# Attention and two expert layers on one core: elementwise work of the weight conversions moved from GpSimd to VectorE and ScalarE

## The chip, the cores and the metric

The kernel runs on one core of a Trainium2 chip. Its time is the device time of one execution in microseconds (us). The engines are TensorE (PE in the profile, PEld for its weight loads), VectorE (DVE), ScalarE (ACT), GpSimd (POOL) and SyncE (SP); each takes its own instructions in order, and they wait for each other by semaphores. All inputs and outputs lie in HBM, working data in SBUF, products of TensorE in PSUM.

## The reference

Three layers follow each other; nothing but their shapes and formulas matters here.

```python
# 1: attention, batch 4, 8 heads, 512 local + 32 global positions, head size 64
s_l = concat(q_l @ k_g.T, where(|i-j| <= 32, q_l @ k_l.T, -1e9)) / 8 ; out_l = softmax(s_l) @ [v_g; v_l]
s_g = q_g @ [k_g; k_l].T / 8                                         ; out_g = softmax(s_g) @ [v_g; v_l]
# 2: 2304 tokens x 512 -> 2048 -> 512;  w_in, w_out arrive as 64-bit floats
h = x @ w_in ; g = h if h >= 1, 0 if h <= -1, else (h+1)**2 / 4 ; x = g @ w_out
# 3: 8 experts, one per token (argmax), only tokens with x @ w_skip > 0
out = x + gate * (relu(x @ w1[e]) @ w2[e])
```

The matrices of layers 2 and 3 are multiplied in three products, high x high, high x low and low x high, where high is a value rounded to TensorE's fast float format (fp32r) and low is what is left.

## The kernel before

**Attention (lines 189 to 441).** 64 steps `s`, eight for each of the 8 pairs of heads. In a step TensorE makes scores ahead (L252), transposes probabilities (L290) and multiplies with the values (L305). VectorE masks and reduces (`reduce_max`, L261), adds, inverts and scales (L275, L279, L284), and copies the output out of PSUM (L308). ScalarE takes exponentials (L268) and copies the transposes (L291). GpSimd copies the columns of the global queries into the transposed tile (`global_columns`, L296). Scores are up to five steps ahead of values. An explicit table, `calls`, says at which step a generator takes its next piece: `globals_` for the global queries of the next pair, and `convert` for a slice of weights.

**Conversion of weights (`convert`, L88 to L106).** `w_in` and `w_out` are 64-bit floats, of which a slice of 128x512 is loaded as pairs of 32-bit words. Each of the 32 conversions (16 slices of either) is a generator with six pieces:

1. SP loads the raw words (L91).
2. ScalarE scales the upper words (L94); VectorE scales and rounds the lower words (L95).
3. VectorE masks the sign (L97), shifts and joins (L98).
4. GpSimd adds the rounded lower words (L101), as integers.
5. ScalarE rounds to the high part (L104).
6. GpSimd subtracts it, which gives the low part (L106).

Eight slices of `w_in` and two of `w_out` are converted in attention, the others in the first unit of layer 2.

**Layer 2 (`stage1`, `middle`, `stage2`, L151, L509, L527; main loop L712).** The tokens are cut into five units of 512, 512, 512, 384 and 256; a unit has 16 steps, one for each slice of 128 of the inner size. Iteration `m` issues `stage1(m)` (12 products, L158), `stage2(m-1)` (12 products in the first three units, L533) and `middle(m)`: ScalarE's relu and square (L513, L514), VectorE's clamp (L517, which reads PSUM), ScalarE's rounding to `gh` (L518) and VectorE's subtraction for `gl` (L522). In unit 0 `middle` also drives the conversions by `advance(age)`, which takes the next piece of every conversion of that age. `conversions(m)` ages all of them by one and starts those of `STARTS`; a conversion does pieces 2 to 4 in the middle of the third iteration after its start, and pieces 5 and 6 one iteration later. Six iterations have two conversions at either age. In each step `stage2` goes over the token tiles `q` and does, for each, two products with `gh` and one with `gl`.

`split_x` (L127) makes the high and low parts of the next unit's tokens: ScalarE rounds (L138), an engine given as an argument subtracts (L139). That is VectorE for units 1 to 4 and GpSimd for unit 0, whose four parts are made in steps 20, 28, 36 and 44 of attention.

**Layer 3 (L734 to the end).** Tokens are routed while layer 2 runs. The rows of an expert's tokens are gathered and scattered by GpSimd's indirect DMAs (L641, L707), in blocks of 256 rows; branches (`tc.If`) leave out blocks and experts without tokens. While an expert's products run, `products` (L823) splits the 16 slices of the next expert's weights with `split` (L630): ScalarE rounds, VectorE subtracts, and for slices 5, 8, 11 and 14 GpSimd does.

Of the kernel before, what the change touches and what calls it, by code (L numbers as in the profile page):

```python
# [7 lines left out]
F32 = mybir.dt.float32  # L8
# [39 lines left out]
def tile_kernel(ctx, tc, q, k, v, w_in, w_out, wsg, w1, w2,  # L48
# [39 lines left out]
    def convert(raw, cvt, src, parts):  # L88
        flat = raw.rearrange("p a b -> p (a b)")
        low, high = raw[:, :, 0], raw[:, :, 1]  # L90
        nc.sync.dma_start(out=flat, in_=src.bitcast(I32))  # L91
        yield
        t = cvt() if callable(cvt) else cvt
        nc.scalar.activation(out=t.bitcast(F32), in_=high.bitcast(F32), func=AF.Copy, scale=2.0 ** -112)  # L94
        nc.vector.tensor_scalar(out=low, in0=low.bitcast(U32), scalar1=2.0 ** -29, scalar2=None, op0=ALU.mult)  # L95
        yield
        nc.vector.tensor_scalar(out=high, in0=high, scalar1=-(1 << 31), scalar2=None, op0=ALU.bitwise_and)  # L97
        nc.vector.scalar_tensor_tensor(out=t, in0=t, scalar=3, in1=high, op0=ALU.logical_shift_left,  # L98
                                       op1=ALU.bitwise_or)
        yield  # L100
        nc.gpsimd.tensor_tensor(out=t, in0=t, in1=low, op=ALU.add)  # L101
        yield
        hi, lo = parts()
        nc.scalar.activation(out=hi, in_=t.bitcast(F32), func=AF.Copy)  # L104
        yield
        nc.gpsimd.tensor_tensor(out=lo, in0=t.bitcast(F32), in1=hi.bitcast(F32), op=ALU.subtract)  # L106

    def convert_in(raw, t, f):
        return convert(raw, t, w_in[:, f, :], lambda: (winH[f], winL[f]))
# [14 lines left out]
    tiles = [(b, j) for b in range(B) for j in range(NJ)] + [None]  # L124
    units = [[0, 1, 2, 3], [4, 5, 6, 7], [8, 9, 10, 11], [12, 13, 14], [15, 16]]

    def split_x(u, part=range(4), low=nc.vector):  # L127
        tl = [tiles[i] for i in units[u]]
        loc = [x for x in tl if x]
        for c in part:  # L130
            o = 0
            pieces = [(xT[loc[0][0]][:, c, loc[0][1]:loc[0][1] + len(loc), 0:128], 128 * len(loc), 128)]
            if len(loc) < len(tl):
                pieces.append((xg[:, c], 128, SG))
            for src, m, w in pieces:
                hv = xh[c][:, o:o + m].rearrange("p (j c) -> p j c", c=w)
                lv = xl[c][:, o:o + m].rearrange("p (j c) -> p j c", c=w)
                nc.scalar.activation(out=hv, in_=src, func=AF.Copy)  # L138
                low.tensor_tensor(out=lv, in0=src, in1=hv.bitcast(F32), op=ALU.subtract)  # L139
                o += m  # L140


# [3 lines left out]
    def wo(hl, f):  # L146
        return (woutH, woutL)[hl][f // 4][:, f % 4, :]
# [24 lines left out]
    def advance(age, n=1):  # L172
        for c in pipe:
            if c[0] == age:
                for _ in range(n):
                    next(c[1], None)
# [12 lines left out]
    with tc.tile_pool(name="att", bufs=1) as a1:  # L189
# [206 lines left out]
        for s in range(NS + 1):  # L396
            n, i8 = divmod(s, 8)
            if s < NS:
                if i8 == 1 and 1 <= n and n + 1 < NG:
                    load(V_b, v, n + 1)  # L400
                if i8 == 3 and n + 2 < NG:
                    load(K_b, k, n + 2)
                    load_q(n + 2)
                transposes(s)
            for r in range(ahead, min(s + AHEAD + 1, ahead + 2, NS + 1)):
                if r < NS:
                    scores(r)
                softmax(r, r - 1)
                if r < NS:
                    exps(r)  # L410
                ahead = r + 1
            if s >= 1:
                values(s - 1)
            for g in calls[s]:
                next(g, None)
            if s % 8 == 4 and 2 <= n < 6:
                split_x(0, [n - 2], nc.gpsimd)
            if s + 2 < NS:
                global_columns(s + 2)

            if s == NS - 13:

                sp2 = wp.tile([128, 2, 512, 2], I32, tag="B2", name="sp2")
                sp2t = sp2[:, 1].rearrange("p a b -> p (a b)")[:, 0:512]
                sp0 = wp.tile([128, 2, 512, 2], I32, tag="B0", name="sp0")
                plan(convert_out(sp0[:, 0], cvts[0], 0), *(NS - x for x in (11, 7, 6, 5, 4, 3)))
                plan(convert_out(sp2[:, 0], sp2t, 1), *(NS - x for x in (12, 5, 4, 3, 2, 1)))
            if s == NS - AHEAD:
                sp3 = wp.tile([128, 2, 512, 2], I32, tag="B3", name="sp3")
                raws += [sp3[:, 0], sp3[:, 1]]  # L430
                h_ps += [bank(i, f"h{i}") for i in range(2)]
                conversions(-2)
            if s == NS - 1:
                sp7 = wp.tile([128, 2, 512, 2], I32, tag="B7", name="sp7")
                raws += [sp7[:, 0], sp7[:, 1]]
                conversions(-1)
            if NS - 4 <= s < NS:
                stage1(0, [s - NS + 4])
# [70 lines left out]
    def middle(m):  # L509
        u, f = divmod(m, NF)  # L510
        n = 128 * len(units[u])
        hp, t, (a, b_) = h_ps[m % 2][:, 0:n], tb[m % 2][:, 0:n], gs(m)
        nc.scalar.activation(out=t, in_=hp, func=AF.Relu, bias=half, scale=0.5)  # L513
        nc.scalar.activation(out=t, in_=t, func=AF.Square)  # L514
        if u == 0:
            advance(4)
        nc.vector.scalar_tensor_tensor(out=t, in0=t, scalar=1.0, in1=hp, op0=ALU.min, op1=ALU.max)  # L517
        nc.scalar.activation(out=a, in_=t, func=AF.Copy)  # L518
        if u == 0:
            advance(4)  # L520
            advance(3)
        nc.vector.tensor_tensor(out=b_, in0=t, in1=a.bitcast(F32), op=ALU.subtract)  # L522
        if u == 0:
            advance(3)
            advance(3)

    def stage2(m):  # L527
        u, f = divmod(m, NF)
        gH, gL = gs(m)
        for q in range(len(units[u])):  # L530
            s = slice(128 * q, 128 * q + 128)
            for k, (lg_, rw) in enumerate(((gH, wo(0, f)), (gH, wo(1, f)), (gL, wo(0, f)))):
                nc.tensor.matmul(y_ps[q], lhsT=lg_[:, s], rhs=rw, start=(f == 0 and k == 0),  # L533
                                 stop=(f == NF - 1 and k == 2))

    def store(u):
        for q, i in enumerate(units[u]):
# [89 lines left out]
        src = (w1, w2)[i // 4][bass.ds(e, 1), :, (i % 4) * 1024:(i % 4) * 1024 + 1024]  # L627
        nc.sync.dma_start(out=raws[i], in_=src.rearrange("a p c -> (a p) c"), cond=cond)

    def split(q, f, raw, low=nc.vector):  # L630
        r = raw[:, 512 * (f % 2):512 * (f % 2) + 512]
        hi, lo = Wt[q][0][f], Wt[q][1][f]
        nc.scalar.activation(out=hi, in_=r, func=AF.Copy)
        low.tensor_tensor(out=lo, in0=r, in1=hi.bitcast(F32), op=ALU.subtract)

    def load_ids(addr):
        nc.gpsimd.dma_start(out=nid, in_=table[bass.ds(addr, BLK), :].rearrange("(s p) c -> p s c", s=2))
# [184 lines left out]

    def products(k, many, pre):  # L823
        q = k % 2
        todo = [(1 - q, f, raws[f // 2], nc.gpsimd if f > 4 and f % 3 == 2 else nc.vector)
                for f in range(NF)] if pre else []

        def splits(n=1):
            for _ in range(n):
                if todo:  # L830
                    split(*todo.pop(0))

        if many:
            nc.vector.tensor_copy(out=cyg_, in_=nyg_)
            for f in range(NEF):
                mm1(q, f)
                if f == 1:
                    load_rows()
                    if pre:
                        prefetch(k + 1, range(4 if k == 0 else 2, 8))  # L840
                if f >= (0 if k == 0 else 5):
                    splits()
            nc.vector.tensor_copy(out=pid, in_=cid[:, :, 0:2])
            for s_ in range(2):
                transpose_rows(s_)
            for s_ in range(2):
                for f in range(NEF):
                    mm2(q, s_, s_, f)
                    if f % 2 == 1:
                        splits()  # L850
                if s_ == 0:
                    finish_rows(0)
                    send_rows(0)
        else:
            nc.vector.tensor_copy(out=cyg_[:, 1], in_=nyg_[:, 0])
            load_rows()
            if pre:
                prefetch(k + 1, range(4 if k == 0 else 2, 8))
            mm1_few(q, 0)
            splits(1 if k == 0 else 0)  # L860
            mm1_few(q, 1, range(2))
            transpose_few(0)
            mm1_few(q, 1, range(2, 4))
            nc.vector.tensor_copy(out=pid[:, 1], in_=cid[:, 0, 0:2])
            splits()
            for f in range(NEF):
                mm2(q, 0, 1, f)
                if f == 1:
                    transpose_few(1)
                if f in (2, 3):  # L870
                    transpose_rows(f - 2)
                splits(2 if f % 2 == 0 else 1)
        splits(NF)
# [147 lines left out]
```

## Time and profile before

The median of three timed executions is 743.02 us (742.79 to 744.99). The execution that was profiled took 745.22 us, of which the profile spans 743.5.

| engine | busy us | share of the span |
|---|---|---|
| TensorE, products | 690.8 | 93% |
| TensorE, weight loads | 565.2 | 76% |
| VectorE | 438.5 | 59% |
| ScalarE | 366.4 | 49% |
| GpSimd | 183.5 | 25% |

Matmuls are pipelined and their ends are modelled, so a busy TensorE is not one at its peak. The busy time of an instruction runs from its start to its end as recorded, and holds what it spent standing in between. The share of an engine over the whole span hides that the stages differ; attention lasts until about 155 us, the first unit of layer 2 until about 256, and the experts begin at about 564. The chain of waits that ends last has 55% of its time on TensorE, 16% on VectorE, 9% on DMAs and 8% in "issue", which is time in which an engine waited for nothing that the profile shows.

### The profile page before, as it was taken

How to read it: one execution, taken by the hardware profiler on the slowest of the kernel's cores; microseconds unless marked ns; L12 is line 12 of the kernel's file. 1: busy time of each engine (PE TensorE's matmuls, PEld its weight loads, DVE VectorE, ACT ScalarE, POOL GpSimd, SP SyncE). 2: the span in 40 equal slices, each digit the busy share in tenths (PEclk: the TensorE clock that was granted, in tenths of full speed). 3: DMA queues.
4: the chain of work that ended last, by engine and by line, in shares of the span. 5: the costliest groups of instructions: out<-in, count | busy, mean ns of one | idle time of the engine just before them, and what ended most of it. 6: DMA issues, size and time to landing. Idle time of an engine off the chain costs nothing.

```text
span 743.5 us, 11769 instructions
## 1 busy us (share of the span) xinstructions
PE 690.8 (93%) x4081; PEld 565.2 (76%) x4081; DVE 438.5 (59%) x1375; ACT 366.4 (49%) x872; POOL 183.5 (25%) x210
## 2 busy tenths in 40 slices
PE   6999999899788999999999999999999999999743
PEld 4777777678565777788777888889888799988632
DVE  6899999978999643333434344434666574223801
ACT  4878888855545543335433354445664162112501
POOL 2143333446677300000000000110001343222320
PEclk9999999999999999999999999999999999999957
DMA  9756566323441030000300006021301361114510
GB/s 249 238 170 165 180 178 197 114 86 115 140 118 52 0 114 1 0 1 1 113 1 1 1 0 227 1 58 56 115 1 57 96 218 60 58 37 119 195 47 15
DMA packets 28244, 66.85 MB, mean 90 GB/s; under 512 B 3755, under 2 KB 12589, under 8 KB 27108
## 3 DMA queue, kind: packets, MB, share of 16 engines
q1 hardware_dynamic: 25092, 58.41, 25.2%
q0 software_dynamic: 3040, 7.10, 3.2%
q8 instruction: 51, 0.84, 0.5%
q14 instruction: 61, 0.50, 0.2%
HBM read 53.38 MB, written 12.43 MB: 89 GB/s over the span
## 4 chain that ended last, share of the span: by engine, by line
PE 55%; DVE 16%; DMA 9%; issue 8%; ACT 3%; POOL 2%; POOLq 0%; DVEq 0%; ACTq 0%
PE h L158 21%; PE y L533 21%; DMA nyg<-ys,nid 6%; PE e L663 4%; PE z L698 3%; DVE P_a L284 3%; DVE gl L522 2%; DMA out_dram<-ob,pid 2%; PE o L305 1%; DVE P_a L261 1%; DVE sp L95 1%; ACT P_a L268 1%; PE t L290 1%; DVE cvt L98 1%; DVE cvtm L98 1%
## 5 line engine op out<-in xcount | busy, mean ns | idle before, releaser
L533 PE MATMUL y<-wout,gh 128*128 128x512 f32 x544 | 173.9, 401 | 2.6 <-ACT gh L518 2.5
L533 PEld LDWEIGHTS y<-wout,gh 128*128 128x128 f32 x544 | 100.3, 191 | 25.1 <-ACT gh L518 5.3
L158 PE MATMUL h<-xh,winH 128*128 128x512 f32 (+2 forms) x320 | 118.6, 370 | 0.0
L533 PE MATMUL y<-wout,gl 128*128 128x512 f32 x272 | 109.0, 401 | 7.9 <-DVE gl L522 7.8
L158 PE MATMUL h<-xh,winL 128*128 128x512 f32 (+2 forms) x320 | 114.8, 359 | 0.0
L158 PE MATMUL h<-xl,winH 128*128 128x512 f32 (+2 forms) x320 | 114.5, 358 | 0.0
L517 DVE SCALAR_TENSOR_TENSOR tb<-tb,h 128x512 f32<-128x512 f32 (+2 forms) x80 | 48.5, 606 | 102.9 <-ACT tb L514 102.2
L500 POOL DMA_INDIRECT table<-ids,slot x17 | 17.4, 1024 | 301.7 <-DVE slot L498 298.8
L513 ACT ACTIVATE tb<-h,misc 128x512 f32<-128x512 f32 (+2 forms) x80 | 49.6, 620 | 78.4 <-PE h L158 66.1
L522 DVE TENSOR_TENSOR gl<-tb,gh 128x512 fp32r<-128x512 f32 (+2 forms) x80 | 59.5, 743 | 47.5 <-ACT gh L518 47.4
L533 PEld LDWEIGHTS y<-wout,gl 128*128 128x128 f32 x272 | 51.8, 190 | 23.6 <-DVE gl L522 12.5
L158 PEld LDWEIGHTS h<-xh,winH 128*128 128x128 f32 x320 | 60.3, 188 | 11.0 <-issue 2.7
L518 ACT ACTIVATE gh<-tb 128x512 fp32r<-128x512 f32 (+2 forms) x80 | 45.2, 565 | 44.6 <-DVE tb L517 44.6
L158 PEld LDWEIGHTS h<-xh,winL 128*128 128x128 f32 x320 | 60.3, 189 | 7.9
L158 PEld LDWEIGHTS h<-xl,winH 128*128 128x128 f32 x320 | 60.5, 189 | 7.4
L268 ACT ACTIVATE P_a<-P_a,st 128x160 f32<-128x160 f32 x128 | 53.7, 421 | 22.1 <-DVE st L261 20.9
L698 PE MATMUL z<-WA,h 128*128 128x512 f32 x240 | 57.9, 394 | 0.0
L305 PE MATMUL o<-PT,V 128*64 128x160 f32 x512 | 49.5, 314 | 4.1 <-ACT PT L291 1.9
L698 PEld LDWEIGHTS z<-WA,h 128*128 128x128 f32 x240 | 44.2, 188 | 8.7
L663 PE MATMUL e<-yTH,WA 128*128 128x256 f32 x256 | 48.7, 286 | 0.2
L252 PE MATMUL s<-K,Q 128*128 128x160 f32 x256 | 46.5, 305 | 1.2 <-DVE st L261 0.7
L514 ACT ACTIVATE tb<-tb 128x512 f32<-128x512 f32 (+2 forms) x80 | 45.5, 568 | 2.5
(203 smaller groups left out, 1204.2 us busy)
## 6 DMA issues: line engine op xcount, KB each, us to landing
xr<-in_w_dram SPq DMA_DIRECT2D x24, 512.0 KB, 6.6
V<-in_v_dram SPq DMA_DIRECT2D x8, 1024.0 KB, 4.9
K<-in_k_dram SPq DMA_DIRECT2D x7, 800.0 KB, 5.7
raw<-in_w_in_dram SPq DMA_DIRECT2D x10, 512.0 KB, 6.5
sp<-in_w_out_dram SPq DMA_DIRECT2D x10, 512.0 KB, 3.9
ys<-xT SPq DMA_DIRECT2D x15, 256.0 KB, 2.9
out_dram<-xT SPq DMA_DIRECT2D x15, 256.0 KB, 3.9
Q<-in_q_dram SPq DMA_DIRECT2D x14, 256.0 KB, 7.0
```

Of the source, the lines that this page charges most:

```text
L158: nc.tensor.matmul(hp, lhsT=lw, rhs=rx[:, 0:n], start=(c == 0 and k == 0), stop=(c == 3 and k == 2))
L252: nc.tensor.matmul(s_ps[s % 2][:, a, 0:W], lhsT=Q_b[n % 2][:, i, j, :, :, a].rearrange("p h c -> p (h c)"), rhs=K_b[n % 2][:, i, W * j + 9 ...
L268: nc.scalar.activation(out=px(s, a), in_=px(s, a), func=AF.Exp, bias=st[:, a:a + 1], scale=-1.0, accum_out=st[:, 2 + a:3 + a])
L305: nc.tensor.matmul(o[64 * h:64 * h + 64, 0:W], lhsT=V[:, j, t, i * 128 + h * 64:i * 128 + h * 64 + 64], rhs=PT[:, t, h, :], start=(t == 0) ...
L513: nc.scalar.activation(out=t, in_=hp, func=AF.Relu, bias=half, scale=0.5)
L514: nc.scalar.activation(out=t, in_=t, func=AF.Square)
L517: nc.vector.scalar_tensor_tensor(out=t, in0=t, scalar=1.0, in1=hp, op0=ALU.min, op1=ALU.max)
L518: nc.scalar.activation(out=a, in_=t, func=AF.Copy)
L522: nc.vector.tensor_tensor(out=b_, in0=t, in1=a.bitcast(F32), op=ALU.subtract)
L533: nc.tensor.matmul(y_ps[q], lhsT=lg_[:, s], rhs=rw, start=(f == 0 and k == 0), stop=(f == NF - 1 and k == 2))
L663: nc.tensor.matmul(hp, lhsT=lw, rhs=ry[:, c], start=(n == 0), stop=(n == 11))
L698: nc.tensor.matmul(z_ps[z], lhsT=lh[:, d], rhs=rw, start=(f == 0 and k == 0), stop=(f == NEF - 1 and k == 2))
```

## The change

In `convert`, the rounding of the lower words goes from VectorE to ScalarE, the addition and the subtraction from GpSimd to VectorE. The subtractions of `split_x` and `split` that were GpSimd's go to VectorE. In `middle` the pieces of the conversions are put in another order: pieces 5 and 6 of the older ones stay ahead of the subtraction for `gl`, pieces 2 to 4 of the younger ones all come behind it. `stage2` does all products with `gh` of a step first, and those with `gl` after them.

```diff
@@ convert
-        nc.vector.tensor_scalar(out=low, in0=low.bitcast(U32), scalar1=2.0 ** -29, scalar2=None, op0=ALU.mult)
+        nc.scalar.activation(out=low, in_=low.bitcast(U32), func=AF.Copy, scale=2.0 ** -29)
...
-        nc.gpsimd.tensor_tensor(out=t, in0=t, in1=low, op=ALU.add)
+        nc.vector.tensor_tensor(out=t, in0=t, in1=low, op=ALU.add)
...
-        nc.gpsimd.tensor_tensor(out=lo, in0=t.bitcast(F32), in1=hi.bitcast(F32), op=ALU.subtract)
+        nc.vector.tensor_tensor(out=lo, in0=t.bitcast(F32), in1=hi.bitcast(F32), op=ALU.subtract)
@@ split_x
-    def split_x(u, part=range(4), low=nc.vector):
+    def split_x(u, part=range(4)):
...
-                low.tensor_tensor(out=lv, in0=src, in1=hv.bitcast(F32), op=ALU.subtract)
+                nc.vector.tensor_tensor(out=lv, in0=src, in1=hv.bitcast(F32), op=ALU.subtract)
@@ attention
-                split_x(0, [n - 2], nc.gpsimd)
+                split_x(0, [n - 2])
@@ middle
         nc.scalar.activation(out=a, in_=t, func=AF.Copy)
         if u == 0:
             advance(4)
-            advance(3)
         nc.vector.tensor_tensor(out=b_, in0=t, in1=a.bitcast(F32), op=ALU.subtract)
         if u == 0:
             advance(3)
             advance(3)
+            advance(3)
@@ stage2
-        for q in range(len(units[u])):
-            s = slice(128 * q, 128 * q + 128)
-            for k, (lg_, rw) in enumerate(((gH, wo(0, f)), (gH, wo(1, f)), (gL, wo(0, f)))):
-                nc.tensor.matmul(y_ps[q], lhsT=lg_[:, s], rhs=rw, start=(f == 0 and k == 0),
-                                 stop=(f == NF - 1 and k == 2))
+        for lows in (False, True):
+            for q in range(len(units[u])):
+                s = slice(128 * q, 128 * q + 128)
+                for hl in range(1 if lows else 2):
+                    nc.tensor.matmul(y_ps[q], lhsT=(gL if lows else gH)[:, s], rhs=wo(hl, f),
+                                     start=(f == 0 and hl == 0 and not lows), stop=(f == NF - 1 and lows))
@@ split
-    def split(q, f, raw, low=nc.vector):
+    def split(q, f, raw):
...
-        low.tensor_tensor(out=lo, in0=r, in1=hi.bitcast(F32), op=ALU.subtract)
+        nc.vector.tensor_tensor(out=lo, in0=r, in1=hi.bitcast(F32), op=ALU.subtract)
@@ products
-        todo = [(1 - q, f, raws[f // 2], nc.gpsimd if f > 4 and f % 3 == 2 else nc.vector)
-                for f in range(NF)] if pre else []
+        todo = [(1 - q, f, raws[f // 2]) for f in range(NF)] if pre else []
```

## Rows read from the trace of the kernel before

**Rows 1.** Windows: length, each engine's busy time (instructions), granted clock, DMA share, GB/s.

```profile
34.70:122.20 87.50, 83.08 (x726) 65.06 (x724) 85.12 (x417) 73.26 (x245) 31.48 (x54) 1.00 0.60 170
122.20:155.30 33.10, 30.36 (x245) 22.51 (x239) 29.75 (x120) 23.47 (x70) 15.50 (x22) 0.95 0.41 148
161.50:247.90 86.40, 76.10 (x303) 57.75 (x301) 79.78 (x87) 46.90 (x80) 58.26 (x42) 0.96 0.32 98
247.90:577.00 329.10, 328.83 (x1776) 273.68 (x1777) 144.05 (x462) 152.13 (x302) 24.15 (x23) 1.00 0.13 42
577.00:743.50 166.50, 138.14 (x817) 120.71 (x815) 68.82 (x141) 43.27 (x92) 46.23 (x47) 0.93 0.30 94
```

**Rows 2.** Order of time, VectorE, one iteration: start, duration, line, operands, preceding idle.

```profile
222.02 0.67 DVE L517 SCALAR_TENSOR_TENSOR tb<-tb,h 128x512 f32<-128x512 f32 x1
222.62 2.58 DVE L95 TENSOR_SCALAR sp<-sp 128x512 int32<-128x512 uint32 x2
225.12 1.76 DVE L522 TENSOR_TENSOR gl<-tb,gh 128x512 fp32r<-128x512 f32 x1
...
227.26 0.69 DVE L98 SCALAR_TENSOR_TENSOR cvtm<-cvtm,sp 128x512 int32<-128x512 int32 x1
...
228.33 1.66 DVE L98 SCALAR_TENSOR_TENSOR cvtm<-cvtm,sp 128x512 int32<-128x512 int32 x1
229.91 0.68 DVE L517 SCALAR_TENSOR_TENSOR tb<-tb,h 128x512 f32<-128x512 f32 x1
```

**Rows 3.** Order of time, GpSimd, the same stretch.

```profile
222.18 1.31 POOL L101 TENSOR_TENSOR cvt<-cvt,raw 128x512 int32<-128x512 int32 x1 [0.63 <-DVE cvt L98]
223.45 1.47 POOL L106 TENSOR_TENSOR wout<-cvt,wout 128x512 fp32r<-128x512 f32 x1
224.87 1.46 POOL L106 TENSOR_TENSOR winL<-cvt,winH 128x512 fp32r<-128x512 f32 x1
228.03 1.41 POOL L101 TENSOR_TENSOR cvtm<-cvtm,sp 128x512 int32<-128x512 int32 x1 [1.70 <-DVE cvtm L98]
```

**Rows 4.** Order of time, VectorE: instructions with no GpSimd work beside them.

```profile
55.36 0.51 DVE L284 TENSOR_SCALAR P_a<-P_a,st 128x160 f32<-128x160 f32 x2
...
132.26 0.42 DVE L95 TENSOR_SCALAR raw<-raw 128x512 int32<-128x512 uint32 x1
...
132.99 0.15 DVE L275 TENSOR_SCALAR st<-st 128x2 f32<-128x2 f32 x1
...
252.97 2.48 DVE L139 TENSOR_TENSOR xl<-xT,xh 128x512 fp32r<-128x512 f32 x4
```

**Rows 5.** Groups of VectorE: 34.7 to 155.3 (two), 161.5 to 247.9 (one); busy, mean.

```profile
L284 DVE TENSOR_SCALAR P_a<-P_a,st 128x160 f32<-128x160 f32 x102 | 38.5, 418 | 0.0
...
L275 DVE TENSOR_SCALAR st<-st 128x2 f32<-128x2 f32 x50 | 13.0, 259 | 0.6
...
L522 DVE TENSOR_TENSOR gl<-tb,gh 128x512 fp32r<-128x512 f32 x13 | 18.8, 1444 | 4.5 <-ACT gh L518 4.5
```

**Rows 6.** Order of time, TensorE: first products of two steps; then chain of waits.

```profile
161.50 0.39 PE L158 MATMUL h<-xh,winH 128*128 128x512 f32 x1
...
250.48 0.39 PE L158 MATMUL h<-xh,winH 128*128 128x512 f32 x1
...
329.61 2.72 PE y L533 x12
332.33 2.72 PE h L158 x12
```

**Rows 7.** Order of time: ScalarE in the conversions, TensorE ahead of the last block.

```profile
160.96 1.21 ACT L94 ACTIVATE cvtm<-sp 128x512 f32<-128x512 f32 x2
...
716.19 0.77 PE L678 MATMUL e<-WA,yTH 128*128 128x512 f32 x1 [13.51 <-issue]
```

**Rows 8.** Waits of GpSimd, 34.7 to 155.3: total us, times, longest.

```profile
POOL xl L139 <- ACT xh L138: 22.8, 4, 6.3
...
POOL winL L106 <- ACT winH L104: 14.5, 7, 2.8
```

## Prediction

> **What bounds the kernel now.** I read the busy time by stage first [rows 1]. TensorE is idle 4.4 of 87.5 us in the first (attention), 2.7 of 33.1 in the second (the last heads, where the granted clock is 0.95), 10.3 of 86.4 in the third (the sixteen steps of the first unit, with the weight conversions; clock 0.96) and 0.3 of 329 in the fourth (the other units of the layer). VectorE is busy 97%, 90% and 92% of the first three. So a change that takes load off VectorE can pay there, not in the fourth stretch. The last stretch has 28 us of idle TensorE, to be looked at separately.
>
> VectorE's busy time is not all work, which only the order of time shows. Rows 2 are one heavy iteration of the first unit, from L517 at 222.02 to the next at 229.91, 7.89 us. Two L95 take 2.58 together, L522 takes 1.76 and the second L98 1.66. Their undisturbed prices are 0.42 for L95 [rows 4] and 0.69 for L98 and the like (the L98 at 227.26 in [rows 2]). Rows 3 hold the reason: beside each long instruction GpSimd runs an L101 or L106 of 1.3 to 1.5 us, and the VectorE instruction ends about half a microsecond after GpSimd's, as if it began only then: L95 begun at 222.62 beside 222.18 and 223.45, L522 beside 224.87, L98 beside 228.03. L517, which reads one operand from PSUM, runs in 0.67 beside the L101 at 222.18. So a GpSimd instruction on SBUF operands stops VectorE instructions on SBUF operands for its whole length. In attention L284 and L275 pay: 51 pairs of L284 at the undisturbed 0.51 [rows 4] would be 26.0 us and they take 38.5; 50 L275 at 0.15 [rows 4] would be 7.5 and they take 13.0 [rows 5]. That is 18.0 us of standing, in a stretch with 24 GpSimd products. In the third stretch 13 L522 at 0.69 would be 9.0 and take 18.8 [rows 5].
>
> TensorE's own pace: 12 products of a unit step take 2.72 us, in either layer [rows 6], so an iteration can't be shorter than 5.44.
>
> **The change, part by part.**
>
> *First unit.* In a heavy iteration (two conversions in their middle, two in their end; six of the sixteen) VectorE loses two L95 and gains two additions and two subtractions. The price of a moved one: four like it in a row (L139, both operands in SBUF) take 2.48 [rows 4], so (2.48 - 0.69) / 3 = 0.60 from start to start. The order becomes L517, two subtractions, L522, L97 and L98 twice, two additions: 0.60 + 1.20 + 0.60 + 2 x 1.07 (227.26 to 228.33 in [rows 2]) + 1.20 = 5.74 us. Nothing is left on GpSimd to stop it. ScalarE then issues nine instructions in an iteration instead of seven. L95's two are new to it and no row shows them; from below 0.42, what VectorE asks, from above a 128x512 conversion on ScalarE, a pair of L94 in 1.21 [rows 7]. I take 0.6, nearest to the same operand shape on the same engine. Nine at 0.6 are 5.4 us, so ScalarE is close to TensorE's pace but not over it. The lighter ten iterations have less on both.
>
> So six iterations run at up to 5.74 where TensorE wants 5.44: a lag of 1.8 us at most. It need not reach TensorE. The low half of a step is read one whole iteration after it is begun, and now eight products (8 x 0.227 = 1.8 us) instead of two stand ahead of the first low product. So the reordering of the second layer buys 1.4 us of slack and moves nothing else; it issues the same 12 products. Also on its path: the addition now stands ahead of the next L517 on VectorE, and the subtraction ahead of L522, so both halves of a step wait behind them; that is in the 5.74. The load of the next raw chunk on SP waits for the addition, as before. The DMA engines are busy 32% of this stretch and 60% of attention [rows 1], so the same loads in five sixths of the time, some 40%, have room.
>
> From the first product of step 2 at 161.50 to that of step 15 at 250.48 [rows 6] are 88.98 us; 13 iterations of 5.44 are 70.7. At TensorE's pace the gain is 18.2; with the whole lag 16.4. I take 17.
>
> *Attention.* On VectorE: 24 moved instructions at 0.60 add 14.4, ten L95 at 0.33 (0.42 less the 0.09 by which two such instructions overlap) save 3.3, and the 18.0 of standing go: a net 6.9 less. What is late next is TensorE, which has 4.4 + 2.7 us of idle time to give and 5% of clock over 33.1 us, some 1.7: 8.8 at most [rows 1]. ScalarE's 73.3 of 87.5 become about 77, still below. I take 6.5, with 0 and 8.8 as bounds. The split of x on VectorE now waits for ScalarE's rounding, just ahead of it in the same step; I count four times half a microsecond, inside the 6.5.
>
> *Fourth stretch.* TensorE has 0.3 us of idle. Nothing.
>
> *Experts.* Four of the sixteen splits of an expert move from GpSimd to VectorE. Beside the products they are covered; the one place where they are not is ahead of the last block. There TensorE stands for 13.5 us in front of 716.19 [rows 7] and waits for nothing that the profile shows, well after the splits. I take 0, with 2 either way.
>
> The Trainium skill, page "SBUF — State Buffer", section "SBUF: two separate sides", says that VectorE and GpSimd share a port pair as an exclusive lock for a whole instruction, also for VectorE with two SBUF inputs against a GpSimd instruction that reads SBUF. Rows 2 and 3 agree (1.66 against 0.69). By that rule the moved instructions will in turn meet the global columns' copies that stay on GpSimd; it is the second rival below.
>
> The sum: 17 + 6.5 + 0 + 0 = 23.5 off the profiled execution of 745.22 (span 743.5), so 721.7. That execution lies 2.2 above the median of the timed runs, 743.02; off the median it is 719.5.
>
> **The rivals.**
>
> *The first unit runs at VectorE's durations.* If instructions that depend on each other don't overlap as those four did, a moved one costs 0.69 and an iteration about 6.4; with waits for ScalarE, whose 5.4 is near as well, six iterations lose 1.0 each, 5.8 where the forecast counts 1.2: 724. For it: the four that overlapped did not depend on each other, while an addition follows the L98 that writes its operand. Against: with two conversions interleaved, that L98 is two instructions back, and L98 to L517 steps by 1.58 at a duration of 1.66 in rows 2, overlapped as well.
>
> *Attention gives nothing.* The global columns' copies (L296, one for each step, a quarter of the elements of the instructions of rows 3, so some 0.35 us) stay on GpSimd. If each moved instruction met one, 24 x 0.35 = 8.4 would take back the 6.9: 726. Against: VectorE reads PSUM in half of its attention instructions, and such an instruction is not stopped (0.67 beside 222.18 in [rows 2, 3]).
>
> *VectorE inherits GpSimd's waits; slower.* GpSimd waited 22.8 us for ScalarE ahead of four splits of x and 14.5 ahead of seven subtractions [rows 8]. VectorE takes its instructions in order: if it stood in these waits, reduce_max, the scaling and the evacuation of the outputs would queue behind, and TensorE behind them. 37.3 - 6.9 = 30.4 more, less 5.7 us of idle time of VectorE in the two stretches [rows 1]: 25 more, 17 less in the first unit, 751. It decides from 24 us of new waits of VectorE on ScalarE in attention. Against: GpSimd was there early because it had nothing else; a subtraction comes a whole attention step after its rounding in VectorE's order, and 64 steps share the 155 us ahead of the third stretch, over 2 us each.
>
> *The standing is not GpSimd's doing.* Then the change does not do what it says: 76 instructions (64 of conversions, four of x, eight of two experts) at 0.60 less 32 L95 at 0.33 are 35 us more on VectorE, most of it in stretches where it is busy over 90%: some 765. Against: every long instruction of rows 2 has its partner in rows 3.
>
> *The last stretch shifts.* The program's instructions lie elsewhere after the change, and the idle 13.5 us [rows 7] may grow or shrink. The Trainium skill, page "Runtime: NRT & Kernel Launch", section "Instruction fetch mechanics", says that a taken branch out of the loaded window waits for its code; no row shows what sets that length here. I give it 3 us either way on top, within the range.
>
> **How the numbers follow.** Forecast, 719.5: 0.70, of which its own range is 715 to 724. First unit at durations 0.13, attention without gain 0.09, shifted last stretch beyond the forecast's range 0.03, VectorE inherits the waits 0.03, standing not GpSimd's 0.02. The low end is all bounds together, 743.0 - 18.2 - 8.8 - 2 = 714, and 2 more for the last stretch: 712. The high end takes in the first two rivals and half of both together: 730. About 0.3% is what a measurement of this kernel can tell from no change. Slower gets the two rivals on that side less a part in which gains make up for them, 0.04; within 0.3% 0.02; faster 0.94.
>
> **What would show it.** Right: no L95, L522 or L98 of VectorE over 0.8 us; L517 to L517 between 5.4 and 5.8 in the heavy iterations; TensorE's clock at 1.00 through the first unit; first product of step 15 about 23 us earlier; L284 pairs at 0.51 throughout; the stretch from there to the experts unchanged. Wrong: waits of VectorE on ScalarE in front of L106 and L139 of over a microsecond each; iterations over 6.2; ScalarE over 95% in the first unit; a last stretch that differs by more than 3 us.

## The result, and the profile of the changed kernel

The changed kernel takes 720.29 us (median of 4 runs, 719.69 to 723.25) where the kernel before took 744.0 in the same series (742.79 to 745.64): ratio 0.9688, 95% interval 0.9652 to 0.9723. Another series (r_after below) gave 719.66 against 742.34, ratio 0.9677 (0.9652 to 0.9702). The forecast was 719.5. The profiled execution took 719.69, span 717.6.

The windows by stage, columns as in [rows 1]. The first two are cut at the same times as there, so they hold a little more of the work that follows; the third runs from step 2 of the first unit, which now begins at 156.77, to step 15 at 227.50:

```profile
34.70:122.20 87.50, 84.55 (x733) 65.88 (x730) 82.08 (x432) 76.96 (x255) 12.15 (x41) 1.00 0.59 175
122.20:155.30 33.10, 31.63 (x247) 23.80 (x246) 28.93 (x123) 27.19 (x76) 3.61 (x11) 1.00 0.44 155
156.77:227.50 70.73, 70.73 (x314) 58.58 (x312) 65.98 (x114) 61.36 (x105) 0.00 (x0) 1.00 0.37 119
227.50:554.00 326.50, 326.38 (x1767) 271.62 (x1766) 142.22 (x458) 150.85 (x299) 21.42 (x21) 1.00 0.13 43
554.00:717.60 163.60, 136.14 (x817) 119.80 (x816) 65.21 (x149) 42.38 (x92) 35.70 (x39) 0.93 0.31 96
```

In the third line TensorE (the first busy time) is never idle: thirteen iterations in 70.73 us, 5.44 each, where before they took 88.98 [rows 6]. The clock is 1.00 there and in the second line, where it was 0.96 and 0.95. GpSimd is down to nothing in the third line and to the copies of L296 in the first two. VectorE is still busy 94% of the first line.

The first products of steps 2 and 15, in order of time on TensorE, against [rows 6]:

```profile
156.77 0.39 PE L158 MATMUL h<-xh,winH 128*128 128x512 f32 x1
...
227.50 0.39 PE L158 MATMUL h<-xh,winH 128*128 128x512 f32 x1
```

Step 2 begins 4.73 us earlier, step 15 22.98 earlier. From there the two traces stay parallel: the clamp of VectorE (L517) in iteration m = 18 comes at 250.21 instead of 273.16 (22.95 earlier), the first VectorE instruction of the experts at 543.13 instead of 566.09 (22.96).

One heavy iteration on VectorE, from L517 to L517, beside [rows 2]:

```profile
205.80 0.68 DVE L517 SCALAR_TENSOR_TENSOR tb<-tb,h 128x512 f32<-128x512 f32 x1
206.40 0.69 DVE L106 TENSOR_TENSOR wout<-cvt,wout 128x512 fp32r<-128x512 f32 x1
207.00 0.69 DVE L106 TENSOR_TENSOR winL<-cvt,winH 128x512 fp32r<-128x512 f32 x1
207.61 0.69 DVE L521 TENSOR_TENSOR gl<-tb,gh 128x512 fp32r<-128x512 f32 x1
208.21 0.43 DVE L97 TENSOR_SCALAR sp<-sp 128x512 int32<-128x512 int32 x1
208.67 0.69 DVE L98 SCALAR_TENSOR_TENSOR cvtm<-cvtm,sp 128x512 int32<-128x512 int32 x1
209.28 0.42 DVE L97 TENSOR_SCALAR sp<-sp 128x512 int32<-128x512 int32 x1
209.74 0.69 DVE L98 SCALAR_TENSOR_TENSOR cvtm<-cvtm,sp 128x512 int32<-128x512 int32 x1
210.34 1.28 DVE L101 CUSTOM_DVE_ANT_0 cvtm<-sp,cvtm 128x1024 uint16<-128x1024 uint16 x2
211.55 0.68 DVE L517 SCALAR_TENSOR_TENSOR tb<-tb,h 128x512 f32<-128x512 f32 x1
```

Two more instructions than before (four gained, two lost) and 5.75 us instead of 7.89, because none runs over 0.7. L521 is the line that was L522. A 128x512 instruction with two operands is followed by the next after 0.60 (206.40, 207.00, 207.61). That holds for the additions (L101) too, since with two conversions at least one other instruction stands between each of them and the L98 that writes its operand. In a lighter iteration, with one conversion, the addition comes directly behind its L98:

```profile
163.94 0.69 DVE L98 SCALAR_TENSOR_TENSOR cvt<-cvt,raw 128x512 int32<-128x512 int32 x1
164.78 0.69 DVE L101 CUSTOM_DVE_ANT_0 cvt<-raw,cvt 128x1024 uint16<-128x1024 uint16 x1
```

There the step is 0.84, and it is 0.83 in the three other such places of the first unit: an addition directly behind the instruction whose result it takes does not overlap with it. L97 and the L98 behind it, which takes its result, don't overlap either (0.46 at a duration of 0.42).

ScalarE in the same iteration; its rounding is L95:

```profile
205.92 0.63 ACT L104 ACTIVATE winH<-cvt 128x512 fp32r<-128x512 f32 x1
206.52 0.63 ACT L518 ACTIVATE gh<-tb 128x512 fp32r<-128x512 f32 x1
207.06 0.66 ACT L94 ACTIVATE cvtm<-sp 128x512 f32<-128x512 f32 x1
207.62 0.67 ACT L95 ACTIVATE sp<-sp 128x512 int32<-128x512 uint32 x1
208.18 0.68 ACT L94 ACTIVATE cvtm<-sp 128x512 f32<-128x512 f32 x1
208.74 0.68 ACT L95 ACTIVATE sp<-sp 128x512 int32<-128x512 uint32 x1
209.32 0.68 ACT L513 ACTIVATE tb<-h,misc 128x512 f32<-128x512 f32 x1
```

The steps are 0.54 to 0.60, so the 0.6 of the forecast holds, and ScalarE keeps up.

In attention (34.7 to 155.3) the groups of VectorE that stood are these, against [rows 5], and below them what TensorE and VectorE waited for by name in the same stretch (total us, times, longest):

```profile
L284 DVE TENSOR_SCALAR P_a<-P_a,st 128x160 f32<-128x160 f32 x102 | 27.4, 311 | 0.0
...
L275 DVE TENSOR_SCALAR st<-st 128x2 f32<-128x2 f32 x50 | 8.4, 168 | 0.5
```

```profile
PE g L237 <- DVE Pg L232: 1.7, 3, 0.9
PE o L305 <- issue: 1.4, 2, 1.1
PE o L305 <- POOL PT L296: 1.2, 5, 0.3
...
DVE xl L139 <- ACT xh L138: 1.8, 4, 0.5
```

38.5 became 27.4 and 13.0 became 8.4: 15.7 us of standing are gone in these two groups. The wait for the rounding of x that VectorE took over is 1.8 us in four times, where GpSimd had stood 22.8 in the same place [rows 8].

### The profile page after: what moved, and what is told of

Its sections match the earlier page's. It is cut to its first block, busy times and chain, and to the rows that moved or that the text cites. A ratio compares the mean times of both kernels' runs of the same rounds, so it can differ in the third digit from the quotient of the medians.

```text
span 717.6 us, 11768 instructions
## 1 busy us (share of the span) xinstructions
PE 678.9 (95%) x4081; PEld 562.0 (78%) x4081; DVE 411.9 (57%) x1419; ACT 382.7 (53%) x904; POOL 80.7 (11%) x134
## 4 chain that ended last, share of the span: by engine, by line
PE 71%; DMA 8%; issue 6%; DVE 5%; ACT 1%; POOL 1%; POOLq 0%; DVEq 0%
PE y L534 26%; PE h L158 26%; DMA nyg<-ys,nid 6%; PE e L664 5%; PE z L699 3%; PE o L305 3%; PE t L290 2%; PE s L252 2%; DMA out_dram<-ob,pid 2%; PE r L465 1%; DVE P_a L261 1%; ACT P_a L268 1%; DVE P_a L284 1%; PE r L469 1%; DMA nid<-table 1%
## 5 line engine op out<-in xcount | busy, mean ns | idle before, releaser
L534 PE MATMUL y<-wout,gh 128*128 128x512 f32 x544 | 139.9, 396 | 0.1
L517 DVE SCALAR_TENSOR_TENSOR tb<-tb,h 128x512 f32<-128x512 f32 (+2 forms) x80 | 48.5, 607 | 105.4 <-ACT tb L514 104.8
L534 PE MATMUL y<-wout,gl 128*128 128x512 f32 x272 | 74.9, 390 | 0.0
L521 DVE TENSOR_TENSOR gl<-tb,gh 128x512 fp32r<-128x512 f32 (+2 forms) x80 | 48.9, 611 | 41.9 <-ACT gh L518 41.6
L268 ACT ACTIVATE P_a<-P_a,st 128x160 f32<-128x160 f32 x128 | 53.8, 423 | 15.3 <-DVE st L261 14.4
```

What stands on the lines that cost most here:

```text
L268: nc.scalar.activation(out=px(s, a), in_=px(s, a), func=AF.Exp, bias=st[:, a:a + 1], scale=-1.0, accum_out=st[:, 2 + a:3 + a])
L534: nc.tensor.matmul(y_ps[q], lhsT=(gL if lows else gH)[:, s], rhs=wo(hl, f), start=(f == 0 and hl == 0 and not lows), stop=(f == NF - 1 and ...
```

## The experiments

All were run on the chip beside the kernel before. Its median was 742.43 in the first series (e1 to e4), 742.34 in the second (r_after, e5 to e7), 742.22 in the third (e8 to e10) and 742.12 in the last (e11). Where a trace is compared, the mark is L517 of iteration m = 18, at 273.16 before and at 250.21 after: from there 312.28 us pass to the first finished row block of the experts in every kernel, within 0.02.

**Theory and rivals.** Theory: a GpSimd instruction on SBUF operands stops VectorE's instructions on SBUF operands, so removing it makes VectorE, and behind it TensorE, faster. Rivals: it was the latency of the two-engine chain that went; it was the order of the products; it was the rounding's move alone. The new order of the pieces in `middle` was not run by itself.

**e1: the order alone.** The kernel before with the new order of the second layer:

```diff
-        for q in range(len(units[u])):
+        for lows in (False, True):
+            for q in range(len(units[u])):
```

> The kernel before with nothing changed but the second layer's order (all products with gh first, those with gl last). Theory (GpSimd's instructions stop VectorE's): the stops stay, the heavy iterations stay at 7.9 us from L517 to L517, the time stays within 1 us of before's 744. Rival (the order is what pays): the 7.5 us that TensorE waits for gl in the first unit go, 736 to 737.

Measured 741.97, ratio 0.9993 (0.9979 to 1.0007). The heavy iterations still step by 7.89 (L517 at 220.97, 228.86, 236.75). The order by itself buys nothing while VectorE is the bound.

**e2 and e3: one stage each.** The change in the first unit alone (e2) and in attention alone (e3), by a flag:

```diff
-        nc.gpsimd.tensor_tensor(out=t, in0=t, in1=low, op=ALU.add)
+        add = nc.vector if new else nc.gpsimd
+        add.tensor_tensor(out=t, in0=t, in1=low, op=ALU.add)
```

> The kernel before with the change in the first unit of layer 2 alone (conversions begun there, their order, the second layer's order); attention's conversions and splits and the experts' splits stay on GpSimd. Theory: the first unit runs at TensorE's pace, heavy iterations at 5.74, 18.2 us less than before, 725 to 727. Rival (the two stages share their gain, for instance because a quicker attention alone lets the conversions start ahead): less than 14 us off.

> The kernel before with the change in attention alone (ten conversions and four splits of x). Theory: 4.7 us off, what the two traces show between the start of the second step's first product, 739 to 740. Rival (VectorE is the bound of attention, and the 6.9 us less load on it count in full): 737.

e3: 737.58, ratio 0.9938 (0.9917 to 0.9959), 4.85 us; step 2 begins at 156.78 and the mark comes 4.75 earlier, as in the changed kernel; the heavy iterations stay at 7.9. e2: the heavy iterations step by 5.74 and the mark comes 18.26 earlier, but the time is 727.09 (726.18 to 727.95), 15.3 below before. The stage behaves as expected; 3 us come back in the last stretch, taken up in e10 and e11.

**e4: idle work for GpSimd.** The changed kernel, with two unread GpSimd subtractions added to each conversion of the first unit. They feed nobody, so no chain grows longer:

```diff
+        for d in dummy:
+            for _ in range(2):
+                nc.gpsimd.tensor_tensor(out=d, in0=hi.bitcast(F32), in1=hi.bitcast(F32), op=ALU.subtract)
```

> The changed kernel with two more GpSimd subtractions of 128x512 for each conversion of the first unit, issued when its high part is there, into a tile that nobody reads; nothing waits for them. Theory (a GpSimd instruction on SBUF operands stops VectorE's): four in a heavy iteration, 1.3 us each, bring L517 to L517 from 5.74 to 8 or more, and 10 to 22 us come back, 730 to 742. Rival (before lost its time to the longer chain of add, round, subtract through GpSimd, not to stops): within 1 us of 720.

Measured 749.1 (747.68 to 749.83), ratio to before 1.0089 (1.006 to 1.0119): all of the gain and 6.7 us more are lost. L517 steps by 8.87. VectorE in order of time, then GpSimd beside it:

```profile
207.63 0.68 DVE L523 SCALAR_TENSOR_TENSOR tb<-tb,h 128x512 f32<-128x512 f32 x1
208.23 1.28 DVE L111 TENSOR_TENSOR wout<-cvt,wout 128x512 fp32r<-128x512 f32 x1
209.43 1.52 DVE L111 TENSOR_TENSOR winL<-cvt,winH 128x512 fp32r<-128x512 f32 x1
210.88 1.52 DVE L527 TENSOR_TENSOR gl<-tb,gh 128x512 fp32r<-128x512 f32 x1
212.32 1.26 DVE L99 TENSOR_SCALAR sp<-sp 128x512 int32<-128x512 int32 x1
213.62 0.69 DVE L100 SCALAR_TENSOR_TENSOR cvtm<-cvtm,sp 128x512 int32<-128x512 int32 x1
```

```profile
207.92 2.49 POOL L109 TENSOR_TENSOR yt<-wout 128x512 f32<-128x512 f32 x2 [3.49 <-ACT wout L106]
210.48 2.81 POOL L109 TENSOR_TENSOR yt<-winH 128x512 f32<-128x512 f32 x2
```

Four VectorE instructions that took 0.69 or 0.42 in the changed kernel take 1.26 to 1.52 beside four GpSimd ones, and the fifth, after GpSimd has ended at 213.29, takes 0.69 again. The iteration grows by 8.87 - 5.74 = 3.13 us for four GpSimd instructions, 0.78 each. This is the stop shown by itself, and the latency rival is not needed: nothing reads what was added, and in [rows 2] VectorE had no idle time in which it could have waited for a chain. The expected time (730 to 742) was too low: with 8.87 us an iteration costs 3.43 more than TensorE's pace, and the lag accumulated over the whole of the conversions (the mark 28.35 later than in the changed kernel).

**r_after and e5: the rounding back on VectorE.** The changed kernel once more, and with L95 on VectorE:

```diff
-        nc.scalar.activation(out=low, in_=low.bitcast(U32), func=AF.Copy, scale=2.0 ** -29)
+        nc.vector.tensor_scalar(out=low, in0=low.bitcast(U32), scalar1=2.0 ** -29, scalar2=None, op0=ALU.mult)
```

> The changed kernel once more, beside the next three: 719 to 721.

> The changed kernel with the rounding of the lower words back on VectorE. Theory (VectorE's sum sets the heavy iterations, and TensorE feels only what is beyond its slack): L517 to L517 goes from 5.74 to 6.4 (two L95 at 0.33), six iterations lag by 5.8 us behind TensorE, of which some 3 us of slack are free, so about 3 us more in the first unit and about half a microsecond in attention: 723 to 724. Rival (ScalarE pays for the rounding what VectorE saves, since it is close to TensorE's pace as well): within 1 us of the changed kernel.

r_after 719.66; e5 723.5 (723.25 to 724.79), 3.8 more. VectorE in e5:

```profile
204.05 0.68 DVE L517 SCALAR_TENSOR_TENSOR tb<-tb,h 128x512 f32<-128x512 f32 x1
...
206.46 0.75 DVE L95 TENSOR_SCALAR raw<-raw 128x512 int32<-128x512 uint32 x2
...
210.46 0.68 DVE L517 SCALAR_TENSOR_TENSOR tb<-tb,h 128x512 f32<-128x512 f32 x1
```

Two L95 take 0.75 here, undisturbed (2.58 for two in [rows 2]), and the iteration is 6.41 = 5.74 + 0.67. So once GpSimd's share has moved, the rounding's move is worth 3.8 of the 22.7 us in the timed runs. The time fits the expectation better than the stages do: in the trace step 2 begins at 158.18, 1.4 later than in the changed kernel (half a microsecond was expected), and the mark comes at 256.11, 5.9 later.

**e6: the old order in the changed kernel.**

```diff
-        for lows in (False, True):
-            for q in range(len(units[u])):
+        for q in range(len(units[u])):
```

> The changed kernel with the second layer's products in the old order (two with gh and one with gl for each token tile). Theory (the order only adds 1.4 us of slack, and the lag of the heavy iterations is at most 1.8 us against 1.9 that are left without it): within 1 us of the changed kernel. Rival (the order hides the whole lag): 1.8 us more or beyond, 722 and up, with TensorE waiting for gl in the heavy iterations.

719.54, ratio 0.9691 (0.9668 to 0.9715), the changed kernel's time. In the trace the mark comes at 250.99, 0.8 later, of which 0.4 are there at step 2 (157.13). The order is worth under a microsecond.

**e7: the experts' splits back on GpSimd.**

```diff
-        todo = [(1 - q, f, raws[f // 2]) for f in range(NF)] if pre else []
+        todo = [(1 - q, f, raws[f // 2], nc.gpsimd if f > 4 and f % 3 == 2 else nc.vector)
+                for f in range(NF)] if pre else []
```

> The changed kernel with the experts' splits of slices 5, 8, 11 and 14 back on GpSimd. Theory (they lie beside the products, and the stop ahead of the last block is not theirs): within 1 us of the changed kernel. Rival (the 3 us by which the two parts of the change alone, 15.3 and 4.9, fall short of the whole, 23.2, are the experts'): 723.

718.21 (718.1 to 718.87), within the range of r_after (716.86 to 720.63). In this kernel it does not matter where the splits run: they lie beside the products.

**e8 and e9: what is left of GpSimd in attention.** e8 is the changed kernel without 60 of the 64 copies of L296; e9 has the copies on VectorE:

```diff
-            if s + 2 < NS:
+            if s + 2 < 4:
                 global_columns(s + 2)
```

```diff
-            nc.gpsimd.tensor_copy(out=PT_b[s % 4][:, :, :, 128:W],
+            nc.vector.tensor_copy(out=PT_b[s % 4][:, :, :, 128:W],
```

> The changed kernel with only the first 4 of the 64 GpSimd copies of L296 (the columns of the global queries are then stale in the other attention units: this part of the computation is left out). Shortfall-by-lock theory: the 1.8 us that attention fell short of 6.5 are lost beside these copies, so step 2 starts at about 155.0 instead of 156.77 and the time is about 718 (717 to 719). Rival, TensorE has become the bound of attention (its idle time in 34.7 to 122.2 us is only about 3 us): step 2 starts at 156.3 to 156.9 and the time is that of the changed kernel within 0.6 us, though VectorE's reductions of L284 (312 ns in the changed kernel) fall to about 260.

> The changed kernel with the copies of L296 on VectorE, so that GpSimd computes nothing in attention. VectorE was busy 82 of 87.5 us there; it gains 41 copies of about 0.2 us and loses what L284 waited (128 times about 0.05 us). Theory that TensorE is the bound: within 1 us of the changed kernel if the two cancel, 2 to 4 us slower if they do not and VectorE becomes the bound. Shortfall-by-lock theory: 718 to 719.

e8: 719.79 (719.65 to 720.25); step 2 begins at 156.01, 0.76 earlier than in the changed kernel, and the time is the same. The standing theory of the shortfall fell; its rival holds, though the step moved slightly more than its bound. The groups of VectorE in 34.7 to 155.3, in e8:

```profile
L284 DVE TENSOR_SCALAR P_a<-P_a,st 128x160 f32<-128x160 f32 x101 | 25.9, 299 | 0.0
L275 DVE TENSOR_SCALAR st<-st 128x2 f32<-128x2 f32 x50 | 8.2, 164 | 1.0
```

Without any GpSimd work beside it L284 takes 25.9 us, so 1.5 of the 27.4 was standing beside L296. (The mean of 299 counts an instruction's whole duration, with the overlap into the next; my "about 260" compared it with half a pair, and was the wrong measure.) e9: 724.47 (723.75 to 725.65), 4.8 above r_after, and step 2 begins at 162.38, 5.6 later. The copies last 220 ns each, 14.0 us by durations, but the next instruction starts 0.13 to 0.14 after them, and 1.6 of standing go: up to step 2 VectorE is busy 143.80 us where it was 138.44 in the changed kernel, 5.4 more. The loss is above both expectations, and all of this work reaches step 2: attention in the changed kernel has almost no spare time on VectorE. GpSimd is the right place for these small copies.

**e10 and e11: where e2's 3 us went.** e10 is e2 again. e11 is e10 with the experts' splits on VectorE too, which is the changed kernel with attention alone as before:

```diff
-        todo = [(1 - q, f, raws[f // 2], nc.gpsimd if f > 4 and f % 3 == 2 else nc.vector)
+        todo = [(1 - q, f, raws[f // 2], nc.vector)
```

> The kernel of e2_first_unit once more, unchanged. It was 15.3 us faster than before where its last iteration of the first unit (m = 18) came 18.3 us earlier. If the missing 3 us are the variation of the last stretch between executions, it comes out now at 724 to 725.5 (18 below the kernel before); if they belong to this build, at 726 to 728 again, with 470 to 472 us behind that iteration.

> The changed kernel with attention alone as before (its conversions, the split of x inside it), or: e10_first_unit_again with the experts' splits 5, 8, 11, 14 on VectorE too. Its iteration m = 18 should come at 254 to 255 us, as in e10. If e10's 3 us over 724 come from the experts' splits on GpSimd, this takes 723.5 to 725; if they belong to the combination of an old attention with the new first unit, 726.5 to 728.5; if they are a property of each build, nothing is fixed, between 723 and 729.

e10: 727.72 (726.4 to 731.75), as e2; so it belongs to the build, not to chance. e11: 724.35 (723.59 to 724.87), close to the 723.2 that its mark asks for, 18.9 us earlier than before's. So in this pair the kernel with the experts' splits on GpSimd takes 3.4 us more, and in e7, with the new attention, the same edit costs nothing. All kernels keep pace to the first finished block (312.28 after the mark); from the last but one block to the last they take 28.6 us in e7, 29.3 in the changed kernel, 30.7 in e11, 31.5 in r_after, 32.1 in e2 and 33.3 in e10. The changed kernel and r_after are the same program, so 2.2 us of such a distance can differ between two executions; it is the timed ranges that set e2 and e10 (726.18 to 731.75) apart from e11. The stall that the profile names, TensorE's wait for "issue" ahead of the last block, in the changed kernel, in e7 and in e11:

```profile
691.47 0.77 PE L679 MATMUL e<-WA,yTH 128*128 128x512 f32 x1 [13.03 <-issue]
```

```profile
690.46 0.77 PE L679 MATMUL e<-WA,yTH 128*128 128x512 f32 x1 [12.39 <-issue]
```

```profile
695.80 0.77 PE L683 MATMUL e<-WA,yTH 128*128 128x512 f32 x1 [13.58 <-issue]
```

It is 12.85 in e10, the slowest of them, so this stall does not account for the differences. Another one does: VectorE's wait for "issue" ahead of its last instruction, behind TensorE's last product, in e10 and in e11:

```profile
719.55 0.75 DVE L708 SCALAR_TENSOR_TENSOR ob<-z,pid,cyg 128x512 f32<-128x512 f32 x1 [10.51 <-issue]
```

```profile
717.97 0.75 DVE L708 SCALAR_TENSOR_TENSOR ob<-z,pid,cyg 128x512 f32<-128x512 f32 x1 [8.10 <-issue]
```

It is 11.29 in e2 and between 7.60 and 8.16 in every other run, e7 and the kernel before (8.16) included. So the 2.4 to 3.2 us are lost there, more than 20 us behind the last split (it ends at 684.83 in e10), and not in the splits' own work. What VectorE waits for there the profile does not show (only in the changed kernel, where it is 7.99, does it name TensorE's sequencer), and why it lasts longer in this build stays open.

## Why the prediction came out

**The mechanism** was right: GpSimd's instructions on SBUF operands stopped VectorE's. e4 shows it without a change of any dependency, and e1 and e5 take the order and the rounding out of the account. The Trainium skill, "SBUF — State Buffer", section "SBUF: two separate sides", describes it as an exclusive lock on a shared port pair for the whole of an instruction; the trace agrees (from 0.69 to as much as 1.52 in e4).

**First unit, 17 forecast, 18.25 measured** (22.98 - 4.73; e2's mark: 18.26). The iteration came out as worked out, 5.74. The step that was mis-sized is the lag: 1.2 us were taken off for six iterations of 5.74 against 5.44, and none of it reached TensorE, which ran all thirteen at 5.44. Even with the old order (e6) it was about 0.4. With iterations of 6.41 (e5) the lag does reach it.

**Attention, 6.5 forecast, 4.73 measured** (e3: 4.85 in time). The windows from the start to the first product of step 2, before and after, columns as in [rows 1]:

```profile
0.00:161.50 161.50, 147.74 (x1188) 113.04 (x1189) 145.86 (x688) 124.06 (x400) 54.88 (x99) 0.99 0.61 178
```

```profile
0.00:156.77 156.77, 145.62 (x1189) 111.97 (x1190) 138.44 (x700) 128.10 (x410) 23.57 (x75) 1.00 0.60 184
```

VectorE's load fell by 7.4 us (145.86 to 138.44), where 6.9 had been counted. The two parts of that count were off in opposite directions. In the groups of [rows 5] 15.7 us of standing went instead of 18.0: 1.7 stand beside the copies of L296 that stay on GpSimd (27.4 and 8.4 in the changed kernel, 25.9 and 8.2 in e8), and 0.6 comes mainly from the reference for L275, 0.15 in one place and 0.164 on the average in e8. About 2 us more went where none had been counted: two L97 and two L95, one of each beside GpSimd, that took 3.6 us where four undisturbed ones take 1.7. The step that was mis-sized is the last one, that TensorE gains nearly all of it (6.5 of 6.9): 4.73 of the 7.4 reach step 2, and the rest is new idle time of VectorE (15.6 us before, 18.3 after, 1.8 of them in front of L139 and 1.1 more in front of L261, which waits for TensorE's scores). e8 shows the same: paying the 1.7 back brings only 0.76 at step 2 and nothing measurable in the time. TensorE keeps some 2.6 us of idle time in the first stretch (84.90 of 87.50 busy in e8), which the forecast had counted as its to give. And 4.73 is itself near the upper end: with the old attention step 2 begins between 160.50 (e1) and 161.50 (before) in five traces, with the new one between 156.57 (e4) and 157.13 (e6) in six, 4.2 us apart on the average. One sign named for the case of being right did not come: L284's pairs are not at 0.51 throughout, 51 of them take 27.4 us.

**Fourth stretch, 0:** right, 22.98 at step 15 and 22.96 at the first expert.

**Experts and last stretch, 0 with 2 and 3 either way:** the timed gain is 22.7 in the series of r_after and the gain at the mark 22.95, so on the median nothing was added. The profiled executions differ by 25.5 because the one of before (745.22) lay above its median; that was allowed for in the sum. The rival of a shifting last stretch is no idle one: e2 and e10 pay 3 us there. One reading ahead of this was wrong: the 13.51 us ahead of the last block do not lie well after the splits. In the kernel before TensorE's wait begins at 702.68, and VectorE's last split (L634) ends at 705.69.

**The rivals.** VectorE did not inherit GpSimd's waits: 1.8 us in front of L139, none named in front of L106, against the 24 at which that rival decided. The first rival's iteration of 6.4 did not come (5.74), but its premise was right: a dependent addition directly behind its L98 steps by 0.83, even more than the rival's 0.69. It decided nothing because in the heavy iterations another instruction always stands between the two, which was the argument against it. The two errors of the sum, 1.25 too little and 1.8 too much, nearly cancel: 23.5 forecast, 22.7 to 23.7 measured. That the total is met within a microsecond is in part luck.

## What to carry to other kernels

Before giving GpSimd a share of VectorE's work, look at VectorE's instructions beside it in order of time: if the same instruction takes twice as long there, GpSimd's share is being paid by VectorE, 0.78 us for each 128x512 instruction here, more than the 0.60 that VectorE needs to do it itself. Price a moved instruction by the step from start to start, not by its duration, and keep another instruction between it and the one whose result it takes (0.60 so, 0.83 without). Small GpSimd copies that take little of this time can be left there: moving L296 to VectorE lost 4.8 us, because VectorE was full.

## What had not been expected of the hardware

- What idle work on another engine can cost: four unread GpSimd subtractions in an iteration took the kernel from 719.66 to 749.1, above the kernel before, though nothing reads their result.
- The integer addition L101 runs on VectorE as a custom instruction on 128x1024 uint16 elements, in 0.68 us and with the same step of 0.60 as a float one on 128x512, as long as it does not come directly behind the instruction whose result it takes (0.83).
- The length of the last stretch depends on the build: 726 to 732 us in e2 and e10 where the mark asks for 724, though nothing that the change touches lies there but four splits for each of two experts, which cost nothing in e7. The excess lies in VectorE's wait ahead of its last instruction (10.5 to 11.3 us instead of 7.6 to 8.2), for which the profile of these two names no cause.
